# A gated state-space and feed-forward kernel: mirrored half of the forward transform taken from odd rows times -2, taps selected across column tiles, a third product buffer, PSUM banks given out by use, finer first loads, and a new order

## The chip, the cores and the metric

The kernel runs on one core of one Trainium2 chip. A core has five engines with a queue of instructions each: TensorE (PE, matrix products into PSUM), VectorE (DVE), ScalarE (ACT, functions from tables, copies, scalings), GpSimd (POOL) and SyncE (SP, here only transfers). An engine works through its own queue in order; engines wait for each other through semaphores. The metric is the device time of one execution in microseconds (us), less is better; a median of 3 runs is given.

## The reference

```python
x = A_u                                           # 1 x 2048 x 512, bf16
g = sigmoid((x * gate_w).sum(-1, keepdims=True))
# A: state-space convolution
dt = exp(log_dt)[:, None]
P = exp((dt * A)[:, :, None] * l)                 # A complex, D=512, N=128; l rounded to bf16
K = einsum("dn,dnl,dn->dl", C, P, dt * B).real    # one filter of 2048 taps per channel
a = irfft(rfft(pad(x)) * rfft(pad(K)))[:L] + x * Dskip
# B: the two rows with the largest x @ w_r go through a gated feed-forward layer (F = 1792)
y = (silu(x_sel @ w_gate) * (x_sel @ w_up)) @ w_down * sigmoid(r_sel)
b = x with y added at those two rows
out = g * a + (1 - g) * b
```

## The kernel before

The convolution is done in blocks of 1024 tokens with transforms written as matrix products. The 512 channels are worked in two halves, h = 0 and 1, of 256; tokens in two blocks, 0 and 1.

- **Parameters and tables.** The six parameter arrays are transposed on PE (`ptr`, line 612), and DVE makes from them the exponents `AL`, the angles `B16`, and the weights `WW` (this needs `PBR`, an eviction, line 494). `exps1` and `exps2` (lines 645 and 649) are exponentials on ACT for both halves. `trig` (line 654) makes four angles at a time: four scalings into integer arguments (`SCL`, line 498), a sine on ACT, an integer add (line 668), a cosine on ACT, and in `tab1` a negation. Arguments and sines each have two buffers. `tab1` and `tab2` (lines 674, 684) are done once per half; `tab2` ends with 12 products of 768 or 1792 columns.
- **Routing.** `routing` (line 717) transposes all tokens in 8 steps (line 724, evicted by line 494 as `XT`), computes gate and routing logits, picks two rows, and runs the feed-forward layer.
- **Forward transform.** `forward` (line 835): per block four frequency tiles `ft`. A first pass (`pm` 0) sums 4 even and 4 odd row tiles, an eviction follows, and a second pass (`pm` 1) adds four matmuls into the same PSUM with a matrix that is the odd one times -2 (`NG`, loaded eight times, 256 KB each), so that the mirrored frequencies come out; a second eviction follows.
- **Filter taps.** `kgen` (line 856) multiplies tables into taps `KA` in groups of six (one PSUM bank each), then selects taps with 32-column matmuls into `KC`. `kspec` (line 903) transforms the taps to `KK`.
- **Products and inverse.** `products` (line 929) multiplies the spectra on DVE, 2048 or 1024 columns at a time; block 1 also needs block 0's spectrum, and its products are written over the block's own spectrum (`xv(1)`). `inverse` (line 960) transforms back, line 992 scales, and SP stores.

Operations that two engines can do (`SCL`, `EV`, the add, the last scaling) are created with both variants, ACT first, except the add, which has DVE first. The string `ORDER` holds three characters per operation, its number in base 36, for all operations in a global order; each engine's queue is that order cut down to its own operations. The string `SECOND` holds a 0 or a 1 per operation; `fixed` (line 179) takes the engine from it:

```python
        for k, i in enumerate(seq):
            o = self.ops[i]
            if o.alt is not None:
                e = list(o.alt)[int(second[i])]
```

`emit` then derives each wait from what was read and written, for buffers that share memory too. PSUM's eight banks have fixed roles: two pairs for `forward` and `kspec`, two banks for `kgen`, two for the rest.

## Time and profile before

| | |
|---|---|
| median of 3 runs | 172.38 us (172.3 to 172.5) |
| span of the profiled execution | 170.1 us (its own time is not given; the median stands 2.3 us above its span) |
| DVE busy | 154.1 us, 248 instructions |
| PE busy | 149.8 us, 1686 matmuls |
| ACT busy | 123.8 us, 196 instructions |
| moved by DMA | 20.12 MB |
| ACT at work without larger gaps | 7.56 to 88 us |
| first DVE work, last DVE product's end | 6.84 us, 162.4 us |

The profile is one execution, taken by the hardware profiler. Its first part gives each engine's busy time, its share of the span and the number of instructions. The second cuts the span into 40 slices; a digit is the busy share of a slice in tenths. The chain follows the work that ended last back from the end, step by step, to what released it. Groups are rows of line, engine, operation, output and input shapes, count, busy time, mean time of one in ns, and idle time in front with what ended it. Many operations are recorded at the line of the helper that makes them: line 479 is `TT` (two tensors on DVE), 494 `EV` (evictions), 498 `SCL`, 490 `AC` (functions on ACT), 501 `DMA`. In a timeline the columns are start and length in us. Instructions of one engine overlap a little, so the step from start to start is shorter than a row's mean.

### The profile page before, as it was taken

The page shows a single profiled execution, that of the slowest core. Times are in us where ns is not written, and L with a number is a line of the kernel's source. Part 1 is how long each engine was busy: PE and PEld are TensorE (multiplying, and loading weights), DVE is VectorE, ACT ScalarE, POOL GpSimd, SP SyncE. Part 2 cuts the span into 40 slices and gives each one's busy share as a digit, 9 for nine tenths or more (in the row PEclk, how much of TensorE's full clock was granted, in tenths as well). Part 3 has the DMA queues.
Part 4 walks back from the last instruction along what each step waited for, and adds up shares of the span by engine and source line. Part 5 has one row for each costly group of instructions (what it writes and reads, how often), then busy time and mean ns, then how long its engine had stood idle before and what let it go on. Part 6 is the DMA issues. An engine that isn't in the chain of part 4 may idle for free.

```text
span 170.1 us, 3961 instructions
## 1 busy us (share of the span) xinstructions
PE 149.8 (88%) x1686; PEld 106.4 (63%) x1686; DVE 154.1 (91%) x248; ACT 123.8 (73%) x196; POOL 3.2 (2%) x8
## 2 busy tenths in 40 slices
PE   0607899989998999999988999999999999969980
PEld 0506674435753444778536779957888887858870
DVE  0399999999999999999999999999999999999931
ACT  2499999999999999999995567755765434506152
POOL 0002000000000000000000000030000000000000
PEclk9999999999999999999999999999999999999998
DMA  4999999273001101103904000049000020020514
GB/s 102 283 388 404 402 409 381 91 241 127 0 5 61 62 11 55 42 24 89 394 14 126 1 2 4 4 85 401 21 4 0 0 62 4 21 72 0 162 57 123
DMA packets 13411, 20.12 MB, mean 118 GB/s; under 512 B 1993, under 2 KB 9034, under 8 KB 13266
## 3 DMA queue, kind: packets, MB, share of 16 engines
q1 hardware_dynamic: 11906, 19.48, 32.5%
q10 hardware_dynamic: 1488, 0.40, 1.2%
q8 instruction: 13, 0.21, 0.5%
q14 instruction: 4, 0.03, 0.1%
HBM read 17.77 MB, written 2.10 MB: 117 GB/s over the span
## 4 chain that ended last, share of the span: by engine, by line
DVE 44%; ACT 23%; PE 22%; issue 6%; DMA 2%; SPq 0%
DVE AR L479 38%; ACT AR L490 14%; PE ps L850 9%; ACT AR L494 5%; PE ps L915 5%; PE ps L867 3%; DVE AR L494 2%; DMA AR<-c_bf 2%; ACT L255 2%; DVE AR L498 2%; PE ps L984 2%; PE ps L815 2%; ACT AR L498 1%; DVE AR L668 1%; DVE AR L488 1%
## 5 line engine op out<-in xcount | busy, mean ns | idle before, releaser
L479 DVE TENSOR_TENSOR AR<-AR 128x2048 bf16<-128x2048 bf16 (+8 forms) x138 | 118.2, 902 | 1.2
L494 ACT ACTIVATE AR<-ps 128x1024 bf16<-128x1024 f32 (+5 forms) x57 | 44.4, 803 | 19.0 <-PE ps L915 7.6
L490 ACT ACTIVATE AR<-AR 128x512 bf16<-128x512 f32 (+4 forms) x74 | 51.1, 753 | 2.5 <-DVE AR L479 1.9
L850 PE MATMUL ps<-AR 128*128 128x512 bf16 x192 | 44.3, 379 | 0.6 <-ACT AR L494 0.5
L984 PE MATMUL ps<-AR 128*128 128x256 bf16 x256 | 30.8, 273 | 2.0 <-DVE AR L479 1.9
L850 PEld LDWEIGHTS ps<-AR 128*128 128x128 bf16 x192 | 18.0, 99 | 22.2 <-issue 2.5
L984 PEld LDWEIGHTS ps<-AR 128*128 128x128 bf16 x256 | 24.8, 98 | 5.9 <-DVE AR L479 3.0
L992 ACT ACTIVATE AR<-ps,AR 128x256 bf16<-128x256 f32 x31 | 13.5, 473 | 18.5 <-PE ps L984 18.1
L915 PE MATMUL ps<-AR 128*128 128x256 bf16 x160 | 19.8, 273 | 0.7 <-ACT AR L494 0.7
L867 PEld LDWEIGHTS ps<-AR 128*128 128x128 bf16 x512 | 18.6, 98 | 1.3 <-ACT AR L494 0.3
L867 PE MATMUL ps<-AR 128*128 128x84 bf16 (+1 forms) x512 | 19.0, 198 | 0.1
L915 PEld LDWEIGHTS ps<-AR 128*128 128x128 bf16 x160 | 15.0, 98 | 5.3 <-ACT AR L494 2.3
L724 PE MATMUL ps<-AR 128*128 128x128 bf16 x64 | 7.7, 309 | 5.8 <-DVE AR L479 5.0
L498 DVE TENSOR_SCALAR AR<-AR 128x256 int32<-128x256 f32 (+1 forms) x38 | 11.0, 315 | 0.0
L724 PEld LDWEIGHTS ps<-AR 128*128 128x128 bf16 x64 | 6.3, 140 | 7.1 <-issue 6.3
L498 ACT ACTIVATE AR<-AR 128x256 int32<-128x256 f32 (+1 forms) x24 | 9.2, 438 | 0.0
L612 PE MATMUL ps<-AR 128*128 128x128 bf16 x24 | 2.9, 312 | 5.8 <-DMA AR<-c_bf 5.8
L971 PE MATMUL ps<-AR 128*128 128x256 bf16 x32 | 7.8, 273 | 0.1
L972 PE MATMUL ps<-AR 128*128 128x256 bf16 x32 | 7.7, 273 | 0.0
L479 DVE TENSOR_TENSOR AR<-AR,ps 128x512 f32<-128x512 bf16 x2 | 1.3, 684 | 6.8 <-PE ps L612 6.8
L494 DVE COPY AR<-ps 128x1024 bf16<-128x1024 bf16 x9 | 6.6, 743 | 0.4 <-PE ps L724 0.3
L612 PEld LDWEIGHTS ps<-AR 128*128 128x128 bf16 x24 | 2.4, 145 | 6.1 <-DMA AR<-c_bf 5.8
(49 smaller groups left out, 91.8 us busy)
## 6 DMA issues: line engine op xcount, KB each, us to landing
AR<-c_ksp SPq DMA_DIRECT2D x5, 512.0 KB, 4.9
AR<-in_A_u_dram SPq DMA_DIRECT2D x2, 1024.0 KB, 8.5
AR<-c_fwdn SPq DMA_DIRECT2D x8, 256.0 KB, 3.7
AR<-c_fwd SPq DMA_DIRECT2D x4, 512.0 KB, 11.4
AR<-c_inv SPq DMA_DIRECT2D x1, 2048.0 KB, 7.7
out_dram<-AR SPq DMA_DIRECT2D x16, 128.0 KB, 2.2
AR<-in_B_w_up_dram SPq DMA_DIRECT2D x1, 1792.0 KB, 15.4
AR<-in_B_w_gate_dram SPq DMA_DIRECT2D x1, 1792.0 KB, 17.9
```

The source lines that it names most:

```text
L479: return P.op(DVE, lambda h: h.tensor_tensor(out=o, in0=a, in1=b, op=op), rd, wr, cost=tt_cost(o, a, b), **k)
L490: return P.op(ACT, lambda h: h.activation(out=o, in_=a, func=func, scale=scale, bias=bias), rd, wr, cost=0.185 + nel(o) * 0.833e-3 + (0.09 ...
L494: return P.op((ACT, DVE), (lambda h: h.activation(out=o, in_=a, func=ACTF.Copy), lambda h: h.tensor_copy(o, a)), rd, wr, cost=(0.185 + n * ...
L498: return P.op((ACT, DVE), (lambda h: h.activation(out=o, in_=a, func=ACTF.Copy, scale=c), lambda h: h.tensor_scalar(out=o, in0=a, scalar1= ...
L724: last = h.transpose(bb(0, 128, db * 256 + t_ * 128, (1, 128)), U(0, 128, (2 * q + t_) * D + db * 128, (1, 128)), IDN(0, (1, 128)))
L850: last = h.matmul(o, w, U(0, 128, (blk * 8 + st * 2 + par) * D, (1, D)), start=(pm + par + st == 0), stop=(par == 1 and st == 3), skip_gro ...
L867: last = hh.matmul(pb(0, 128, (g - b0) * W4 + o, (1, n)), TP[h][1 - i // 2](0, 128, g * 128, (1, 128)), r[i](0, 128, g * n, (1, n)), start ...
L915: last = hh.matmul(pb(0, 128, n * 256, (1, 256)), KP[u](0, 128, tau * 128, (1, 128)), KC[h](0, 128, jg * 256, (1, 256)), start=(k == 0 and ...
L971: hh.matmul(pb(0, 128, e * 256, (1, 256)), DG(0, 128, tb[e] * 128, (1, 128)), U(0, 128, tb[e] * D + h * HC, (1, HC)), start=(e == 0), stop ...
L972: last = hh.matmul(pb(0, 128, e * 256, (1, 256)), OHR(0, 128, tb[e] * 128, (1, 128)), ZB(0, 128, h * HC, (1, HC)), start=False, stop=False)
L984: last = hh.matmul(pb(0, 128, e * 256, (1, 256)), G(0, 128, ((par * 2 + part) * 4 + ft) * 512 + (2 * t2 + e) * 128, (1, 128)), X(0, 128, h ...
L992: P.op((ACT, DVE), (lambda hh, o=o, i_=i_, g_=g_: hh.activation(out=o, in_=i_, func=ACTF.Copy, scale=g_), lambda hh, o=o, i_=i_, g_=g_: hh ...
```

## The change

- **Forward.** The `NG` matrices and their eight loads go. Instead `UO` holds the odd row tiles of a block times -2, made by one `SCL` of 2048 columns per block, and the second pass multiplies the odd matrix `F` with it. Evictions are as before.
- **Tap selection.** The loop over the four column tiles is moved inside, so that neighbouring matmuls go to different column tiles. `sel3` goes: its eight matmuls become part of `sel2` and write into its bank. `kgen` evicts two banks at a time (1008 columns, 6 evictions per half instead of 11).
- **Products.** Products for block 1 no longer overwrite `xv(1)`: each has a buffer of its own, from four places (h = 0) or five (h = 1).
- **Places.** A new class `Life` stands for one use of a PSUM bank, an argument or sine buffer or a product buffer; the string `PLACES` says which one it gets, and `fixed` adds waits between successive uses.
- **First loads.** U comes in four loads instead of two. The gate weights come as two contiguous loads on SP's queue and are transposed on PE (`w8`), where two element-wise loads on ACT's queue brought them; a DVE copy follows.
- **Smaller ones.** The down projection is turned round (56 matmuls of 2 columns for 14 of 512), with a small copy and four transposes behind it. The exponential of zero is a memset on POOL. `DG` reads its scale in pairs.
- **Order.** `ORDER` and `SECOND` are new (643 operations instead of 654); the list scheduler that had once made them is deleted, and lines 183 to 186 stay as they were.

As the code reads the strings, operations with two engines are placed so:

| operation | before: ACT, DVE | after: ACT, DVE |
|---|---|---|
| arguments, 256 | 23, 31 | 46, 8 |
| integer adds, 1024 / 768 | 4, 10 / 2, 0 | 3, 11 / 0, 2 |
| negations, 1024 | 1, 7 | 6, 2 |
| `XT` evictions, 1024 | 0, 8 | 7, 1 |
| `PBR` eviction, 1024 | 0, 1 | 1, 0 |
| forward evictions, 1024 | 12, 4 | 15, 1 |
| x(-2), 2048 | none | 1, 1 |
| `KA` evictions | 21, 1 | 10, 2 |
| `KC` / `KK` evictions | 6, 0 / 16, 0 | 5, 1 / 16, 0 |
| last scaling, 256 | 31, 1 | 29, 3 |

```diff
+class Life:
+    def __init__(self, prog, pool, n, home, region, name):
...
+        self.unit = int(PLACES[k], 36) if k < len(PLACES) else 0
+        self.base, self.c0 = home(self.unit)
+        self.alias = region.alias if region is not None else []
...
+            at[i] = k
             order[o.eng].append(o)
...
 SECOND = (
-    "000000000000000000000000000000001000000000000000000000000000000000000000000000000001010101010101010000000000000000000000000000000000000000000000000000"
...
+    "000000000000000000000000000010000000000000000011001011011100110011100000101010000000010000000000000000000000000000000000000000000000000010100000101000"
+    "001011001001001000010010000000000100100000000101010000000000000011001001000001010000000100000000010000000000000000000000000001001000000000000000000000"
+    "001000000101001000010000001101010000000000000000010110000000000000000000001000000000000000000000000000000000000000000000000000000000000000000000000000"
     "000000000000000000000000000000000000000000000000000000000000000000000000000000000000000000000000000000000000000000000000000000000000000000000000000000"
...
+    "0000000000000000000000000000000100010100000"
+)
+PLACES = (
+    "002423114301111116067020011001126404066110011002421322011010010110010446000024606464021213003203021666446420013427241030132344032571064"
 )
...
+        used = {}
+        for l in self.lives:
+            for u in range(l.unit, l.unit + l.n):
+                used.setdefault((l.pool, u), []).append(l)
+        for ls in used.values():
+            ls.sort(key=lambda l: min(at[i] for i in l.all))
+            for a, b in zip(ls, ls[1:]):
+                assert max(at[i] for i in a.all) < min(at[i] for i in b.all), "a place is held twice"
+                for i in b.all:
+                    self.ops[i].deps.update(a.all)
...
-        NG = [B("ng%d" % i, oF + 16 * KB + 2 * i * KB, 2 * KB) for i in range(2)]
+        UO = B("uo", oF + 16 * KB, 4 * KB)
...
-        PQ = [[B("p%d%d" % (i, h_), o + 4 * i * KB, 4 * KB) for i in range(2)] for h_, o in enumerate((oTI[0], oI))]
+        PQR = [B("pq%d" % h_, o, n * KB) for h_, (o, n) in enumerate(((oTI[0], 16), (oI, 20)))]
+        def place(pool, region, off, nbytes, dt=BF):
+            def home(u):
+                a = AR[:, (off + u * nbytes) // 2:(off + (u + 1) * nbytes) // 2]
+                return (a if dt == BF else a.bitcast(dt)), 0
+            return Life(P, pool, 1, home, region, pool)
...
-            DQ([(U(0, 128, j * 8 * D, (2 * D, 4), (1, 2 * D)), dr(A_u, 1024 * j * D, (2 * D, 128), (256 * D, 4), (1, 2 * D)))], [], [(U, (t, h_)) for t in range(8 * j, 8 * j + 8) for h_ in range(2)], 1048576)
+            for k in range(2):
+                DQ([(U(0, 128, (j * 8 + k * 4) * D, (2 * D, 2), (1, 2 * D)), dr(A_u, (1024 * j + 512 * k) * D, (2 * D, 128), (256 * D, 2), (1, 2 * D)))], [], [(U, (t, h_)) for t in range(8 * j + 4 * k, 8 * j + 4 * k + 4) for h_ in range(2)], 524288)
...
-                if j == 0:
-                    DQ([(NG[ft](0, 128, 0, (1, 1024)), ngsrc(ft))], [], [NG[ft]], 262144)
-        P.op(ACT, ld_w, [], [WL], cost=1.0, n=2, nbytes=20000, dma=True, prio=2.5e5)
+        for i, w in enumerate((gate_w, B_w_r)):
+            DQ([(W8(4 * i, 4, 0, (1, 128)), dr(w, 0, (128, 4), (1, 128)))], [], [(W8, i)], 1024)
...
+            w8 = misc(True)
+            P.op(PE, lambda h: h.transpose(w8(0, 128, 0, (1, 8)), W8(0, 8, 0, (1, 128)), CB(0, 8, 0, (1, 8))), [(W8, 0), (W8, 1), CBI], [w8], cost=0.25)
+            CP(WL(0, 128, 0, (1, 8)), w8(0, 128, 0, (1, 8)), [w8], [WL])
...
-            yb = misc()
+            yb, yt = misc(), misc(True)
             def dn(h):
-                for fb in range(14):
-                    last = h.matmul(yb(0, 2, 0, (1, D)), HB(0, 128, 3 * 28 + fb * 2, (1, 2)), WD[fb // 8](0, 128, fb % 8 * D, (1, D)), start=(fb == 0), stop=(fb == 13))
+                for db in range(4):
+                    for fb in range(14):
+                        last = h.matmul(yb(0, 128, db * 2, (1, 2)), WD[fb // 8](0, 128, fb % 8 * D + db * 128, (1, 128)), HB(0, 128, 3 * 28 + fb * 2, (1, 2)), start=(fb == 0), stop=(fb == 13))
-            P.op(PE, dn, [(HB, 3), *WD], [yb.buf], cost=14 * 0.226)
-            CP(HY(0, 2, 0, (1, D)), yb(0, 2, 0, (1, D)), [yb.buf], [HY])
-            TS(ZB(0, 2, 0, (1, D)), HY(0, 2, 0, (1, D)), RTS(0, 2, 37, (1, 1)), MUL, [HY, K("rs"), (ZB, None)], [(ZB, "y")])
+            P.op(PE, dn, [(HB, 3), *WD], [yb], cost=56 * 0.0255)
+            CP(YT(0, 128, 0, (1, 8)), yb(0, 128, 0, (1, 8)), [yb], [YT])
+            def ytr(h):
+                for db in range(4):
+                    last = h.transpose(yt(0, 2, db * 128, (1, 128)), YT(0, 128, db * 2, (1, 2)), IDN(0, (1, 128)))
+            P.op(PE, ytr, [YT, CBI], [yt], cost=0.3)
+            TS(ZB(0, 2, 0, (1, D)), yt(0, 2, 0, (1, D)), RTS(0, 2, 37, (1, 1)), MUL, [yt, K("rs"), (ZB, None)], [(ZB, "y")])
...
+                SCL(UO(0, 128, 0, (1, 4 * D)), U(0, 128, (blk * 8 + 1) * D, (2 * D, 4), (1, D)), -2.0, uk(*range(blk * 8 + 1, blk * 8 + 8, 2)), [UO])
                 for ft in range(4):
-                    k = blk * 4 + ft
-                    ng = NG[k % 2]
-                    if k > 1:
-                        DMA([(ng(0, 128, 0, (1, 1024)), ngsrc(ft))], [], [ng], 262144, prio=2e5)
-                    pb = fwp[k % 2]
+                    pb = psum(2)
                     for pm in range(2):
                         for part in range(2):
-                            def fw(h, blk=blk, ft=ft, pm=pm, pb=pb, ng=ng, part=part):
+                            def fw(h, blk=blk, ft=ft, pm=pm, pb=pb, part=part):
                                 last = None
                                 o = pb(0, 128, part * 512, (1, 512))
                                 for par in range(pm, 2):
                                     for st in range(4):
-                                        w = ng(0, 128, (st * 2 + part) * 128, (1, 128)) if pm else F(0, 128, ft * 2048 + ((par * 4 + st) * 2 + part) * 128, (1, 128))
-                                        last = h.matmul(o, w, U(0, 128, (blk * 8 + st * 2 + par) * D, (1, D)), start=(pm + par + st == 0), stop=(par == 1 and st == 3), skip_group_check=(pm == 1))
+                                        w = F(0, 128, ft * 2048 + ((par * 4 + st) * 2 + part) * 128, (1, 128))
+                                        x = UO(0, 128, st * D, (1, D)) if pm else U(0, 128, (blk * 8 + st * 2 + par) * D, (1, D))
+                                        last = h.matmul(o, w, x, start=(pm + par + st == 0), stop=(par == 1 and st == 3), skip_group_check=(pm == 1))
                                 return last
-                            P.op(PE, fw, ([ng] if pm else [(F, ft)]) + uk(*range(blk * 8, blk * 8 + 8)), [(pb.buf, part)], cost=(8 - 4 * pm) * 0.217)
...
-            for b0 in range(0, 64, 6):
-                ng = min(6, 64 - b0)
-                pb = kgp[(b0 // 6) % 2]
+            for b0 in range(0, 64, 12):
+                ng = min(12, 64 - b0)
+                pb = psum(1 + (ng > 6))
                 W4 = 4 * NJ
-                def mm(hh, b0=b0, ng=ng, pb=pb):
...
+                for g0 in range(0, ng, 6):
+                    def mm(hh, b0=b0, gs=range(g0, min(ng, g0 + 6)), pb=pb):
+                        last = None
+                        for g in gs:
+                            for i in range(4):
+                                n, o = (W4, 0) if i % 2 == 0 else (4 * NR, 4 * NOF)
+                                last = hh.matmul(pb(0, 128, g // 6 * 512 + g % 6 * W4 + o, (1, n)), TP[h][1 - i // 2](0, 128, (b0 + g) * 128, (1, 128)),
+                                                 r[i](0, 128, (b0 + g) * n, (1, n)), start=(i == 0), stop=(i == 3))
+                        return last
+                    P.op(PE, mm, [*TP[h], *r], [(pb, g0)], cost=min(6, ng - g0) * 4 * 0.0343)
+                d = ((512, ng // 6), (1, 6 * W4)) if ng > 6 else ((1, ng * W4),)
+                EV(KA[h](0, 128, b0 * W4, (1, ng * W4)), pb(0, 128, 0, *d), [pb], [(KA[h], b0)])
...
                 def sel(hh, bk=bk, pb=pb):
                     last = None
-                    for k in range(4):
+                    for c4 in range(4):
+                        for k in range(4):
+                            last = hh.matmul(pb(32 * k, 32, c4, (256, 2), (4, 64)), CB(0, 128, c4, (4, 32)), ka(c4, GROUPS[2 * bk][k], (16, 2)),
+                                             start=(c4 == 0), stop=(c4 == 3 and bk + k > 0), tile_position=(0, 32 * k))
+                    if bk == 0:
                         for c4 in range(4):
-                            last = hh.matmul(pb(32 * k, 32, c4, (256, 2), (4, 64)), CB(0, 128, c4, (4, 32)), ka(c4, GROUPS[2 * bk][k], (16, 2)),
-                                             start=True, stop=(bk + k > 0), tile_position=(0, 32 * k))
-                            if bk + k == 0:
-                                last = hh.matmul(pb(0, 32, c4, (4, 64)), CB(0, 128, 64, (1, 32)), ZB(0, 128, h * HC + c4, (4, 64)), start=False, stop=True, tile_position=(0, 0))
+                            last = hh.matmul(pb(0, 32, c4, (4, 64)), CB(0, 128, 64, (1, 32)), ZB(0, 128, h * HC + c4, (4, 64)), start=False, stop=(c4 == 3), tile_position=(0, 0))
                     return last
...
-            pb, pe = misc(), misc()
+            pb = misc()
             def sel2(hh):
                 last = None
-                for k in range(4):
+                for c4 in range(4):
+                    for k in range(4):
+                        last = hh.matmul(pb(32 * k, 32, c4, (4, 64)), CB(0, 128, c4, (4, 32)), ka(c4, GROUPS[4][k]), start=(c4 == 0), stop=(c4 == 3 and k != 1), tile_position=(0, 32 * k))
+                for k in range(2):
                     for c4 in range(4):
-                        last = hh.matmul(pb(32 * k, 32, c4, (4, 64)), CB(0, 128, c4, (4, 32)), ka(c4, GROUPS[4][k]), start=True, stop=True, tile_position=(0, 32 * k))
...
-            PA, PBb = PQ[h]
+            nbytes = 8 * W
+            tmp = lambda: place("pq%d" % h, PQR[h], (oTI[0], oI)[h], nbytes)
+            halves = lambda b: [(b, 0), (b, 1)]
             for blk in blks:
-                for P_, part in ((PA, 0), (PBb, 1)):
-                    TT(v4(P_), xv(blk), kv(0, part), MUL, kx(blk) + kk(0, part), [P_])
+                pq = [tmp(), tmp()]
+                for part in range(2):
+                    TT(v4(pq[part]), xv(blk), kv(0, part), MUL, kx(blk) + kk(0, part), halves(pq[part]))
                 if blk == 1:
-                    for P_, part in ((PA, 0), (PBb, 1)):
-                        TT(xv(1), xv(0), kv(1, part), MUL, kx(0) + kk(1, part), kx(1))
-                        TT(v4(P_), v4(P_), xv(1), ADD, kx(1), [P_])
-                TT(v1(PA, 0), v1(PA, 0), v1(PBb, 1), SUB, [PBb], [PA])
-                TT(v1(PA, 1), v1(PA, 1), v1(PBb, 0), ADD, [PBb], [PA])
+                    for part in range(2):
+                        t = tmp()
+                        TT(v4(t), xv(0), kv(1, part), MUL, kx(0) + kk(1, part), halves(t))
+                        TT(v4(pq[part]), v4(pq[part]), v4(t), ADD, halves(t), halves(pq[part]))
+                PA, PBb = pq
+                TT(v1(PA, 0), v1(PA, 0), v1(PBb, 1), SUB, [(PBb, 1)], [(PA, 0)])
+                TT(v1(PA, 1), v1(PA, 1), v1(PBb, 0), ADD, [(PBb, 0)], [(PA, 1)])
```

## The prediction

> **What bounds the kernel now.** I read the page's busy table and slices first, then the table by stage, the groups kept apart by shape, the chain, and ACT's timeline.
>
> ```profile
> span 170.1 us, 3961 instructions
> ...
> PE 149.8 (88%) x1686; PEld 106.4 (63%) x1686; DVE 154.1 (91%) x248; ACT 123.8 (73%) x196; POOL 3.2 (2%) x8
> ...
> DVE  0399999999999999999999999999999999999931
> ACT  2499999999999999999995567755765434506152
> ...
> DVE 44%; ACT 23%; PE 22%; issue 6%; DMA 2%; SPq 0%
> ```
>
> DVE is the bound from 6.84 us to 162.4 us. ACT is just as full in the first 21 slices, to about 88 us; its 27% of idle time lies behind that. What goes onto ACT early costs time, what goes onto it late is free.
>
> ```profile
> core 0: us, PE busy (x) PEld busy (x) DVE busy (x) ACT busy (x) POOL busy (x), PEclk, DMA share, GB/s
> ...
> 69.00:88.00 19.00, 18.17 (x310) 12.54 (x307) 18.79 (x31) 18.92 (x31) 0.00 (x0) 1.00 0.35 126
> 88.00:105.40 17.40, 16.66 (x226) 13.04 (x225) 17.32 (x21) 11.00 (x15) 0.00 (x0) 1.00 0.11 32
> ...
> 162.50:170.10 7.60, 3.63 (x32) 3.01 (x32) 0.99 (x2) 3.10 (x7) 0.00 (x0) 0.92 0.26 75
> ```
>
> ACT's timeline gives the step from one instruction to the next: eviction of 1024 0.90 us, sine 0.95, argument 0.31, integer add 0.94.
>
> ```profile
> 43.57 1.00 ACT L494 ACTIVATE AR<-ps 128x1024 bf16<-128x1024 f32 x1
> 44.47 1.04 ACT L490 ACTIVATE AR<-AR 128x1024 bf16<-128x1024 int16 x1
> 45.42 0.40 ACT L498 ACTIVATE AR<-AR 128x256 int32<-128x256 f32 x1
> 45.73 1.04 ACT L668 ACTIVATE AR<-AR 128x1024 int32<-128x1024 int32 x1
> ...
> 84.95 1.78 ACT L490 ACTIVATE AR<-AR 128x1024 bf16<-128x1024 int16 x2
> ```
>
> The last row ends with the last cosine of the second half's tables, at 86.6 us (the next eviction starts at 86.63). Behind it DVE has the rest of that table, then all products, with no gap.
>
> **Where the work lands.** Line 186, which picks the engine of each operation that has two, is not in the diff, so it still reads SECOND by the operation's number. The old string has 59 ones, all on two-engine operations by number. The new one has 61: by number only 22 fall on two-engine operations (171 of 643 are such, so chance gives 16), but by place in ORDER all 61 do. The new string is therefore written by place and read by number, and the engines come out almost at random. Counted through ORDER, ACT gets, up to and with that last cosine:
>
> - arguments 46 instead of 23: 23 x 0.31 = +7.1
> - seven of the eight transposed-input evictions (L494, 1024 from PSUM) that DVE does today: 7 x 0.91 = +6.4, and the P eviction +0.9
> - negations 6 instead of 1: 5 x 0.95 = +4.8
> - forward evictions 14 instead of 9: 5 x 0.91 = +4.6
> - the first new x(-2) of 2048 elements: rows of 256 (411 ns) and 1024 (1056 ns) give 0.84 ns an element, so 1.9, in steps 1.8
> - table evictions: 2 of 1008 (1.8) for 9 of 504 (0.49 steps) and one of 336 (0.4): -3.0
> - adds -1 of 1024 and -2 of 768: -2.5; one exponential less (the memset is on POOL): -0.5
>
> Sum +19.6 us, none of it beside anything: ACT is full there.
>
> **New waits on ACT in that stretch.** (1) The P eviction stands behind seven exponentials (7.56 + 7 x 0.53 = 11.3, done 12.2). DVE's CM2 waits for it, B16 stands behind CM2, and ACT's first argument waits for B16 to 14.0: 1.8. (2) The 12 products of the first half's second table start only when DVE has passed the integer add of a sine that ACT reaches at about 79; they take 10.5, the first two table matmul groups 48 x 0.037 = 1.8, and the eviction that now stands on ACT behind them waits 3.4. (3) Two forward evictions wait for PE, which was held by the down projection and its new transposes: 1.5. (4) Two cosines wait for adds that went to DVE: 0.5 and 1.4. Together 8.6; ends 0 (all caught by slack) and 13 (half as much again). The last cosine ends at 86.6 + 19.6 + 8.6 = 114.8.
>
> **Behind it.** Two table evictions 1.3. Then the three selection groups. Today 16 matmuls of 128 columns are 1.4 us (64 are 5.6), the groups with additions 1.9 and 1.4: 4.7 with no overlap. With neighbours in different column tiles, at best a quarter: 1.2. No row shows it; I take 3.0 and keep both ends. The small eviction ahead of DVE's work went to DVE: 0.4. DVE goes on at 119.5. It still has a cosine product, four of 1024 and a TS, 3.3 in steps; then 8 of 1792 (1.04) and 4 of 768 (0.54), 10.5. Products: today they and DG run from 101.1 to 162.5, 61.4. Dependent neighbours are 1.26 apart (143.74, 145.00, 146.25), independent ones 1.13 (41.46 to 42.59) and 0.61 for 1024. With a third buffer and the new order hardly any neighbours depend on each other: 33 x 1.13 + 32 x 0.61 + 0.8 = 57.5; I take 58.0, ends 57.5 and 61.4. KK evictions stay 2 to 3 us ahead of the products that read them by the same walk, so no wait there. Tail: 162.46 to 170.1 is 7.6; one of the four last inverse groups (32 matmuls 3.67, so 0.9) now stands before DVE's last product: 6.7.
>
> Sum: 119.5 + 3.3 + 10.5 + 58.0 + 6.7 = **198.0 us** of span against 170.1. The profiled execution's own time is not given beyond its span; the median of the runs, 172.38, lies 2.3 above it, so **200.3 us**.
>
> **Parts at nothing.** The eight mirrored-matrix loads (2 MB): no row of PE waits for them; the price if their absence mattered is nil, as DMA was busy for 0.03 to 0.35 between 40 and 105. Four loads of U and two of gate weights (SP, 0.45 each to issue) hide behind ACT's first seven exponentials; w8's transpose blocks the third parameter transpose to about 8.2, still before 11.3 (without that cover the transposes would start some 2 us late, as U's first load takes 7.4 to land today). The down projection: 14 x 0.23 = 3.2 becomes 56 x 0.028 + 0.3, which is on today's chain, but PE then waits for ACT: nothing. The freed HY copy (0.67) and DG's paired reads (0 to -0.6) are on a DVE that waits or are small. PSUM by use: today's PSUM wait, 5.0 before the input transposes, is replaced by the wait for the P eviction. The second x(-2) (on DVE, at most twice the 0.42 of 1024) falls in DVE's idle time. SP's queue: KP's five loads (0.45 each to issue, 4.9 to land) can start when the last forward group is done, about 109, and are in by about 117.5; if they come later, DVE's 13.8 us of table work cover as much. G (7.7 to land) starts when the second half's table matmuls are done, about 142, and is in by 150, ahead of the first inverse group at about 155; without that room each us would hold PE alone. POOL's memset of OHR (1.8) and its load lie in the same gap. ACT's queue loses two gate-weight issues (0.98) that stood before its 3.2 us table load, while DVE's first result at 7.5 still sets its start.
>
> **Rules of the skill.** The trace grants PE a clock of 1.00 in all stages up to 162.5 us. The Trainium skill, "TensorE: Matmul & The Clock Gate" (Part 1), says that about 3.4 us of idleness halve PE's clock until about 3.4 us of work have passed; only the 0.92 of the last stage hints at that here. The Trainium skill, "TensorEngine Tiling (Array Packing)" (Theoretical Speedup), gives up to 4x for 32 columns: by it the sum would be 1.8 lower, by the old rows alone 1.7 higher.
>
> **Rivals.**
> - *Read by place after all*: if the string took effect as it fits, ACT's early load would be as now (31 arguments and all eight evictions on DVE). DVE's sum changes by: forward eviction -1.2, table eviction -0.65, add +0.6, negation +0.35, two x(-2) +1.3, HY and small ones -0.4: 0. Then 172.4 - 3.4 (products) - 0.9 (tail) = 168. Against it: line 186 is not in the diff. 5%.
> - *DVE's relief decides (the other side)*: read by number, DVE has 218 instructions for 248 and about 11 us less. If DVE is the bound throughout, 172.4 - 11 - 3.4 - 0.9 = 157. It decides only if ACT's last cosine ends by 172.0 - (200.3 - 114.8) = 86.5, which is today's 86.6; each us later is a us on the end. ACT would need 28 us of slack in front of 88, and the slices show none. 3%.
> - *PE goes cold*: PE would now idle for stretches of 5 to 12 us. At half clock the first table pair costs +1.8, the selections +3.0: 205. The clock column speaks neither way, as PE had no such gaps. 18%.
> - *A part of the moves hides* (some waits and a third of the moves, 175 to 189): 5%. *More stalls than I found*, such as KK late for the second half: over 213, 7%.
>
> **How the numbers follow.** The forecast as summed has 62%. Low end: no new waits (-8.6), selections 1.2 (-1.8), products 57.5 (-0.5): 189. High end: waits +4.3, selections +1.7, products +3.4, cold PE's rest +3: 213. With the cold case inside, that holds 80%. What a measurement here can tell from no change is 0.2%, 0.35 us. Faster: 5% + 3% = 8%; the same 1%; slower 91%.
>
> **What would show it.** Right: the exponentials end near 48 us instead of 36.8; ACT full to about 115 with some 46 L498-type instructions on it; DVE's busy share well under 80%, its idle time ended by ACT between 35 and 119; products packed from about 133 to 191; ACT nearly idle behind 150. Wrong: DVE as full as now before 100 us, or eight transposed-input evictions on DVE (then the string is read by place); PE's clock at half in many stages (the cold case); a wait of DVE for KK evictions.

## The result and the profile after

The changed kernel takes 206.8 us (median of 4 runs, 206.4 to 207.2) against 172.3 us for the kernel before in the same comparison: a ratio of 1.200, with a 95% interval of 1.198 to 1.203. It is 34.5 us slower; 200.3 had been forecast, with a range of 189 to 213. The profiled execution has a span of 204.8 us against 170.1. An execution that lies over 1.5% above the fastest of its kernel, at a lower clock granted to PE, is left out of the ratios: one of four with extra matmuls in part 2 (209.7 us) and three of four with three classes by place in part 4 (196.9 to 197.8 us).

From the page of the changed kernel: span, busy table, the slices of DVE, ACT and PE's clock, and the shares of the chain.

```profile
span 204.8 us, 4017 instructions
...
PE 152.9 (75%) x1718; PEld 109.7 (54%) x1733; DVE 141.6 (69%) x218; ACT 141.0 (69%) x218; POOL 3.6 (2%) x10
...
DVE  0456010640588679597984846999997999999952
ACT  3566999999889898488999853822686654351153
...
PEclk9999975597599597999999959997999999999999
...
PE 39%; ACT 37%; DVE 18%; issue 2%; DMA 2%; SPq 0%; ACTq 0%; DVEq 0%
```

DVE was at 9 in nearly every slice before. Now it stays at 9 only behind slice 25 (with one 7); ahead of that it has holes, and it is busy 141.6 us for 154.1. ACT has gone from 123.8 to 141.0 us, all of it in front: there it works 20.3 us more (below), behind that 3 us less. The chain's largest share was DVE's 44%; it is now split between PE (39%) and ACT (37%). ACT's part lies almost wholly ahead of 120 us; from 138 us to the end the chain lies on PE nearly throughout.

The line of the engine choice is 137 in this kernel (186 before); `TT` is line 436, `AC` 447, `EV` 451, `SCL` 455, the integer add 610. The next rows are ACT's timeline in the changed kernel (start, length, and in brackets the idle time in front and what ended it).

```profile
14.23 0.42 ACT L455 ACTIVATE AR<-AR 128x256 int32<-128x256 f32 x1 [1.96 <-DVE AR L436]
...
18.78 5.61 ACT L451 ACTIVATE AR<-ps 128x1024 bf16<-128x1024 bf16 x6 [1.70 <-PE ps L666]
...
25.14 9.47 ACT L447 ACTIVATE AR<-AR 128x512 bf16<-128x512 f32 x18
...
49.56 4.37 ACT L455 ACTIVATE AR<-AR 128x2048 bf16<-128x2048 bf16 x7
...
86.99 1.02 ACT L451 ACTIVATE AR<-ps 128x1024 bf16<-128x1024 f32 x1 [2.97 <-PE ps L800]
...
118.49 0.84 ACT L447 ACTIVATE AR<-AR 128x768 bf16<-128x768 int16 x1 [1.48 <-DVE AR L610]
```

The transposed-input evictions stand on ACT in front of 18 exponentials, x(-2) and arguments follow the last exponential at 49.6, and the last cosine ends at 119.3 us, where it ended at 86.6 before. That is 32.7 of the 34.7 us by which the span has grown. Behind it, DVE's timeline:

```profile
124.36 0.42 DVE L451 CAST AR<-ps 128x256 bf16<-128x256 f32 x1 [4.06 <-PE ps L847]
...
128.03 9.97 DVE L436 TENSOR_TENSOR AR<-AR 128x768 bf16<-128x768 bf16 x12
...
155.09 42.04 DVE L436 TENSOR_TENSOR AR<-AR 128x2048 bf16<-128x2048 bf16 x50
```

DVE goes on 5.1 us behind the cosine, starts the 12 table products at 128.03 and ends the last product at 197.13; the remaining 7.7 us are the tail. The same view by stage as before, here from ACT's first exponential to its last cosine (first the kernel before, then the changed one in two rows; the columns are those of the table by stage above):

```profile
7.56:86.63 79.07, 71.83 (x808) 42.88 (x810) 77.67 (x160) 78.81 (x125) 1.17 (x3) 1.00 0.48 177
```

```profile
7.00:49.66 42.66, 22.43 (x185) 13.46 (x185) 14.24 (x46) 38.33 (x64) 0.31 (x1) 0.83 0.61 226
49.66:119.30 69.64, 54.83 (x641) 31.42 (x649) 53.35 (x83) 60.76 (x93) 0.00 (x0) 0.87 0.06 21
```

Before, ACT worked 78.8 of 79.1 us. Now it works 38.3 + 60.8 = 99.1 us of the 111.7 between 7.62 and 119.3: 20.3 us more work, and 12.3 us more waiting.

### The profile page after: what moved, and what is told of

The parts are those of the page before. It is cut to its first block, busy times and chain, and to the rows that moved or that the text cites. A ratio compares the mean times of both kernels' runs of the same rounds, so it can differ in the third digit from the quotient of the medians.

```text
span 204.8 us, 4017 instructions
## 1 busy us (share of the span) xinstructions
PE 152.9 (75%) x1718; PEld 109.7 (54%) x1733; DVE 141.6 (69%) x218; ACT 141.0 (69%) x218; POOL 3.6 (2%) x10
## 4 chain that ended last, share of the span: by engine, by line
PE 39%; ACT 37%; DVE 18%; issue 2%; DMA 2%; SPq 0%; ACTq 0%; DVEq 0%
ACT AR L447 21%; DVE AR L436 15%; PE ps L934 13%; ACT AR L451 7%; ACT AR L455 6%; PE ps L818 6%; PE ps L864 4%; PE ps L800 4%; PE ps L831 2%; DMA AR<-in_A_A_im_dram 2%; PE ps L922 2%; PE ps L921 2%; PE ps L666 2%; ACT AR L610 1%; ACT L217 1%
## 5 line engine op out<-in xcount | busy, mean ns | idle before, releaser
L436 DVE TENSOR_TENSOR AR<-AR 128x1024 bf16<-128x1024 bf16 (+6 forms) x138 | 115.3, 891 | 12.8 <-ACT AR L455 10.3
L451 ACT ACTIVATE AR<-ps 128x1024 bf16<-128x1024 f32 (+6 forms) x56 | 51.4, 956 | 30.4 <-PE ps L871 12.0
L800 PE MATMUL ps<-AR 128*128 128x512 bf16 x182 | 51.2, 440 | 9.7 <-ACT AR L455 7.5
L800 PEld LDWEIGHTS ps<-AR 128*128 128x128 bf16 x192 | 20.5, 111 | 35.1 <-issue 11.8
L934 PE MATMUL ps<-AR 128*128 128x256 bf16 x256 | 29.4, 273 | 0.0
L934 PEld LDWEIGHTS ps<-AR 128*128 128x128 bf16 x256 | 25.0, 98 | 2.9
L942 ACT ACTIVATE AR<-ps,AR 128x256 bf16<-128x256 f32 x29 | 12.3, 474 | 18.7 <-PE ps L934 17.6
L455 ACT ACTIVATE AR<-AR 128x256 int32<-128x256 f32 (+2 forms) x53 | 23.7, 510 | 2.0 <-DVE AR L436 2.0
L818 PEld LDWEIGHTS ps<-AR 128*128 128x128 bf16 x512 | 19.3, 101 | 10.0 <-DVE AR L436 6.9
L864 PE MATMUL ps<-AR 128*128 128x256 bf16 x160 | 18.8, 273 | 0.2 <-ACT AR L451 0.2
L864 PEld LDWEIGHTS ps<-AR 128*128 128x128 bf16 x160 | 15.2, 98 | 3.6 <-ACT AR L451 0.7
L610 DVE TENSOR_SCALAR AR<-AR 128x1024 int32<-128x1024 int32 (+1 forms) x11 | 7.3, 665 | 6.3 <-ACT AR L447 6.3
L831 PE MATMUL ps<-AR 128*32 128x128 bf16 x64 | 4.2, 421 | 6.7 <-ACT AR L451 6.7
L557 PE MATMUL ps<-AR 128*128 128x128 bf16 x24 | 3.1, 310 | 6.1 <-DMA AR<-in_A_A_im_dram 5.8
L921 PE MATMUL ps<-AR 128*128 128x256 bf16 x32 | 7.5, 272 | 0.0
L922 PE MATMUL ps<-AR 128*128 128x256 bf16 x32 | 7.5, 272 | 0.0
L666 PE MATMUL ps<-AR 128*128 128x128 bf16 x64 | 5.7, 265 | 2.3 <-ACT AR L451 2.3
L451 DVE CAST AR<-ps 128x1008 bf16<-128x1008 f32 (+2 forms) x4 | 4.0, 1011 | 4.1 <-PE ps L847 4.1
## 6 DMA issues: line engine op xcount, KB each, us to landing
AR<-in_B_w_up_dram SPq DMA_DIRECT2D x1, 1792.0 KB, 13.8
```

The costliest lines, as they stand in the source:

```text
L436: return P.op(DVE, lambda h: h.tensor_tensor(out=o, in0=a, in1=b, op=op), rd, wr, cost=tt_cost(o, a, b), **k)
L451: return P.op((ACT, DVE), (lambda h: h.activation(out=o, in_=a, func=ACTF.Copy), lambda h: h.tensor_copy(o, a)), rd, wr, cost=(0.185 + n * ...
L455: return P.op((ACT, DVE), (lambda h: h.activation(out=o, in_=a, func=ACTF.Copy, scale=c), lambda h: h.tensor_scalar(out=o, in0=a, scalar1= ...
L666: last = h.transpose(bb(0, 128, db * 256 + t_ * 128, (1, 128)), U(0, 128, (2 * q + t_) * D + db * 128, (1, 128)), IDN(0, (1, 128)))
L800: last = h.matmul(o, w, x, start=(pm + par + st == 0), stop=(par == 1 and st == 3), skip_group_check=(pm == 1))
L818: last = hh.matmul(pb(0, 128, g // 6 * 512 + g % 6 * W4 + o, (1, n)), TP[h][1 - i // 2](0, 128, (b0 + g) * 128, (1, 128)), r[i](0, 128, (b ...
```

## The experiments

Each ratio is to the kernel before, measured beside the kernel in question. Where two experiments are set against each other, I take the difference of their ratios times 172.4 us; the changed kernel's ratio is 1.2003.

**1. Is it the reading of the string?** The string is read by place in `ORDER` instead of by operation number. First throughout, then for the places up to the last cosine alone (the first 376), then for those behind it alone.

```diff
-                e = list(o.alt)[int(second[i])]
+                e = list(o.alt)[int(second[k])]                        # throughout
+                e = list(o.alt)[int(second[k if k < 376 else i])]      # early
+                e = list(o.alt)[int(second[i if k < 376 else k])]      # late
```

> The changed kernel with one index changed: the engine string is read by place in the order, as it fits. Theory (ACT's load ahead of the last cosine sets the end): ACT's last cosine back to 85 to 88 us, DVE the bound again, 166 to 171 us against 172.3 before. Rival A (the parts of the change themselves, such as the x(-2) step, the waits between successive uses of a place or the new order, make half of the loss or more): 188 us or more. Rival B (mostly PE's low clock in gaps): the gaps stay where the new order makes them, 190 to 200.

> The changed kernel, engines by place for the first 376 places of the order (up to and with the last cosine), by number behind it. Theory: nearly all of the loss goes, what is left is table and selection evictions put on DVE behind the cosine, 1 to 4 us: 168 to 174. Rival (the assignment as a whole, late part too): about half way, 185 to 190.

> The other way round: by number up to the last cosine, by place behind it. Theory: the loss stays, 203 to 207 against 206.8 for the change. Rival (the assignment as a whole): about half way, 185 to 190.

Measured: throughout 170.55 us (ratio 0.987, 0.984 to 0.991); early 175.5 (1.019); late 200.9 (1.166). One character of the source is worth 36.7 us of 172.4, and with it the rest of the change leaves the kernel 1.3% below the one before, a small gain whose interval stays below 1. So this kernel beats both, and the loss is the reading of the string and nothing else. The early part is worth 31.2 us, the late part 6.0, together 37.2. The early one came out a little above what had been expected, and the late one was mis-sized (203 to 207 had been expected): two evictions that by number fall to DVE, a table eviction of 1008 and the small one of 256 behind the selections, stand in DVE's queue ahead of the table products. Read by number, these start 8.7 us after the last cosine (119.3 to 128.03), read by place 3.4 us; with the late part alone by place it is 3.4 us too, with the early part alone 8.8. In the kernel read by place, from its timelines of ACT and DVE:

```profile
88.66 2.23 ACT L451 ACTIVATE AR<-ps 128x1008 bf16<-128x1008 f32 x3
```

```profile
15.71 4.27 DVE L451 COPY AR<-ps 128x1024 bf16<-128x1024 bf16 x7
...
92.13 9.97 DVE L436 TENSOR_TENSOR AR<-AR 128x768 bf16<-128x768 bf16 x12
```

The transposed inputs are evicted by DVE, all three remaining table evictions are on ACT, and DVE walks past them to the products.

**2. Is a cold PE part of it?** PE's granted clock in the changed kernel is 0.73 to 0.81 between 20 and 84 us. 97 matmuls of 512 columns, whose results nothing reads, were put into PE's longest waits. The strings were renumbered for these four operations; the engine and the order of all others stay.

```diff
+        for n_ in [34, 30, 7, 26]:
+            pb = psum(1)
+            def warm(h, pb=pb, n_=n_):
+                last = None
+                for _ in range(n_):
+                    last = h.matmul(pb(0, 128, 0, (1, 512)), U(0, 128, 0, (1, 128)), U(0, 128, 0, (1, 512)), start=True, stop=True)
+                return last
```

> The changed kernel with 97 extra matmuls of 512 columns in four of PE's long waits (34 before the first transpose of the routing maximum, 30 before the first mirrored pass, 7 before the down projection, 26 before the selections); they read U and write a free PSUM bank that nothing reads. Theory: PE then runs at full clock where the changed kernel had 0.6 to 0.8, forward evictions come earlier, 2 to 5 us less than the change: 202 to 205. Rival C (the low clock is off the path): 206.3 to 207.5. Rival B (the low clock is most of the loss): under 195.

Measured: the mean clock rises from 0.90 to 0.95, and the time is 205.8 us (205.0 to 206.7; ratio 1.194, 1.188 to 1.200); the span is 203.2 for 204.8. So this warming brought 1.1 us by the ratios (2.5 at the ends of their intervals) and 1.6 in span: below the 2 to 5 that the theory had, with a time between the theory's range and rival C's. PE was not warm throughout, as between 20 and 84 us the clock rose from 0.76 to 0.89 only; what full warmth would bring was not measured. The selections, for which the cold rival had added 3.0 us, show why it is little: their first 32 matmuls take 2.11 us at a clock of 1.00 here, and 2.09 at 0.50 in the changed kernel. The matmuls that do slow down (eight of 512 columns take 3.54 us behind the idle stretch that ends at 38.2 us, and the next eight 1.89) lie where ACT is busy anyway (14.96 of the 15 us from 35 to 50). The Trainium skill, "TensorE: Matmul & The Clock Gate" (Part 1), says that a PE idle for about 3.4 us runs at half clock until it has worked as long; the trace agrees, 0.44 us a matmul behind 9.7 us of idleness and 0.24 later. Not every such gap does it here: in the kernel before PE is idle for 4.99 us until 13.73, and the clock granted behind it is 1.00.

**3. Does each us on ACT count?** One class at a time was set right in the changed kernel: the arguments, or the transposed-input and P evictions.

```diff
-                e = list(o.alt)[int(second[i])]
+                e = list(o.alt)[int(second[k if o.name[0][0] == "arg" and o.cost < 0.4 else i])]                      # arguments
+                e = list(o.alt)[int(second[k if o.name[0][0][:2] == "xt" or o.name[0][0] == "pbr" else i])]           # evictions
```

> The changed kernel with the engine of the arguments alone read by place: 23 of them go from ACT to DVE ahead of the last cosine. Theory (each us of ACT ahead of the last cosine is a us at the end): 23 x 0.31 = 7.1 less, 206.8 to 199.7, between 198 and 202. Rival (ACT only waits longer, as DVE's small operations now stand in front of its integer adds and products): 203 to 208.

> The changed kernel with the engine of the transposed-input evictions and of the P eviction alone read by place: seven and one go back to DVE. Theory: 7 x 0.91 + 0.9 = 7.3 of ACT work and the wait for B16 (2.0) and for the input transposes (1.7) go: 206.8 - 11.0 = 195.8, between 194 and 199. Rival as for the arguments: 203 to 208.

Measured: 204.9 us (ratio 1.185, so 2.7 less) and 203.3 us (1.178, 3.9 less), for 7.1 and 7.3 us of work taken from ACT. The last cosine came 2.0 and 4.1 us earlier. Both times lie in the rival's range. The rule that had carried the forecast, that each us on ACT early is a us at the end, fails here by about half or more. In the first kernel ACT waits 4.45 us for PE at the first table eviction, for 0.66 in the changed one, and 5.8 us for DVE in three places where it had waited 2.1. ACT's timeline of the second kernel shows what replaced the work:

```profile
19.09 1.02 ACT L451 ACTIVATE AR<-ps 128x1024 bf16<-128x1024 f32 x1 [6.27 <-PE ps L800]
```

By number, one eviction of the forward transform (block 0, `ft` 1, first pass; it stands at place 72 of `ORDER`, and by place it is DVE's) stands on ACT in front of 18 exponentials. ACT waits 6.3 us there for a product that PE can only make once the transposes are through. In the changed kernel the wait does not show, because the misplaced input evictions fill that very time.

**4. Three more tests of that.** First three classes at once: arguments, transposed-input and P evictions, negations and x(-2) by place; forward and table evictions and adds still by number. Then the reverse: everything by place except the arguments, and everything except the transposed-input and P evictions.

```diff
-                e = list(o.alt)[int(second[i])]
+                e = list(o.alt)[int(second[k if o.name[0][0][:2] == "xt" or o.name[0][0] in ("pbr", "snc", "uo") or o.name[0][0] == "arg" and o.cost < 0.4 else i])]   # three classes
+                e = list(o.alt)[int(second[i if o.name[0][0] == "arg" and o.cost < 0.4 else k])]                      # all but the arguments
+                e = list(o.alt)[int(second[i if o.name[0][0][:2] == "xt" or o.name[0][0] == "pbr" else k])]           # all but the evictions
```

> The changed kernel, in which the arguments, the input-transpose and P evictions, the negations and the two x(-2) are read by place together; forward and table evictions and the adds stay by number. Counted through ORDER with the steps of the trace of before, this takes 22 us of work from ACT ahead of the last cosine (46.4 to 24.5 in these classes, and by place in full it is 25.2). Arguments alone gave 1.9 and the evictions alone 3.5. Theory A (the loss is shared by several queues, and one class set right only uncovers waits on the next, so that the gains together are much more than their sum): last cosine before 100, 178 to 188. Theory B (the gains simply add, 1.9 + 3.5 + 2 to 3 for the negations and x(-2)): 197 to 200. Theory C (each us of ACT's work counts in full, 22 in all): about 185, last cosine near 97; A and C are told apart by the single moves, which C had at 7.1 and 7.3 and which gave 1.9 and 3.5.

> All read by place, but the arguments by number: ACT gets 23 arguments more ahead of the last cosine, 7.1 us in steps; the rest is as in the kernel read by place throughout (170.55 us). Theory (where ACT is full and the other queues are in step, as before 88 us there, each us put on it counts): last cosine at 94 to 97 instead of 88.75, 175.5 to 178.5. Rival (a class that gave only 1.9 when it was set right alone costs no more when it alone is wrong): 171.5 to 173.5.

> All read by place, but the input-transpose and P evictions by number: seven of eight and the P eviction on ACT, 7.3 us of work in front of and among ACT's exponentials, and DVE's early parameter work then waits for the P eviction behind seven exponentials. Theory: last cosine at 95 to 98, 176.5 to 179.5. Rival (only what it gave when set right alone, 3.5): 173 to 175.

Measured: three classes 193.1 us in the one execution that is compared, 196.9 to 197.8 in the three others; all but the arguments 176.8 (ratio 1.027, 1.022 to 1.031); all but the evictions 181.5 (1.056, 1.050 to 1.061).

The three classes together gained 13.8 us in the execution that is compared (9 to 10 in the others) for 22 us of work. That is short of theory C, the full price, and of theory A, whose last cosine was to come before 100 us and comes at 108.78. Theory B (the gains add) had 197 to 200: the three others lie at its lower end, the compared one 4 us below it. So the full price is not reached; whether the gains only add or come to somewhat more is open. The table by stage, from the first exponential to the last cosine, shows where the rest is. The profile of the second kernel is of the execution that took 196.9 us, so up to 3.8 us of what follows may be its own. First row: read by place throughout; second: three classes by place; third: all but the arguments.

```profile
7.60:88.75 81.15, 72.41 (x821) 42.64 (x829) 77.52 (x164) 77.61 (x119) 0.39 (x1) 0.91 0.35 127
```

```profile
7.80:108.78 100.98, 75.93 (x822) 44.84 (x829) 77.98 (x167) 77.35 (x118) 0.39 (x1) 0.85 0.29 105
```

```profile
7.60:96.10 88.50, 73.07 (x822) 42.02 (x829) 74.00 (x142) 84.48 (x142) 0.31 (x1) 0.90 0.33 119
```

ACT has the same work in the first two, 77.6 and 77.4 us, and DVE too (77.5 and 78.0), and yet the second takes 20 us longer: ACT idles 23.6 us for 3.5. The loss is all waits now, and two rows of ACT's timeline hold 13.6 us of them; the third row is DVE's:

```profile
19.69 1.02 ACT L451 ACTIVATE AR<-ps 128x1024 bf16<-128x1024 f32 x1 [8.05 <-PE ps L800]
...
88.44 1.01 ACT L451 ACTIVATE AR<-ps 128x1008 bf16<-128x1008 f32 x1 [5.59 <-PE ps L818]
```

```profile
32.56 0.17 DVE L441 TENSOR_SCALAR AR<-AR 128x16 bf16<-128x16 f32 x1 [9.38 <-ACT AR L447]
```

The first is the same forward eviction. The exponentials end 9 us later than in the kernel read by place, and DVE, whose next operation reads a result that ACT has behind 18 of them, stands 9.4 us for it. The second is the first table eviction: it waits for PE, PE waits for DVE's table products, and these stand behind everything that DVE does late. A kernel with these forward evictions set right as well was not run, so how much of the 20 us is that one instruction's is open; its own wait is 8.

The reverse tests give the full price, and more. With 23 arguments on ACT, 7.1 us in steps, its busy time rises by 6.9 us (77.6 to 84.5), the last cosine comes 7.3 us later, and the span is 7.3 us longer (176.0 for 168.7); by the ratios it is 6.7 us, inside the 175.5 to 178.5 expected. The evictions cost 11.7 us by the ratios and 10.5 in span for 7.3 us of work, above the 176.5 to 179.5 expected. The rest is two new waits in ACT's timeline of that kernel, 2.05 + 1.13 = 3.2 us for the transposes on PE:

```profile
14.27 1.94 ACT L451 ACTIVATE AR<-ps 128x1024 bf16<-128x1024 bf16 x2 [2.05 <-PE ps L666]
...
17.34 4.69 ACT L451 ACTIVATE AR<-ps 128x1024 bf16<-128x1024 bf16 x5 [1.13 <-PE ps L666]
```

So the same 23 arguments cost about 7 us where all else is in step, and give back 2 to 4 where it is not. The price of a misplaced class is real when it is the only one; several of them stand in each other's shadow.

**5. What are the intended parts worth?** In the kernel read by place, the products of block 1 were again written over the block's own spectrum, with the old order of the six operations and no third buffer. In the changed kernel, the selection loops were put back.

```diff
-                        t = tmp()
-                        TT(v4(t), xv(0), kv(1, part), MUL, kx(0) + kk(1, part), halves(t))
-                        TT(v4(pq[part]), v4(pq[part]), v4(t), ADD, halves(t), halves(pq[part]))
+                        TT(xv(1), xv(0), kv(1, part), MUL, kx(0) + kk(1, part), kx(1))
+                        TT(v4(pq[part]), v4(pq[part]), xv(1), ADD, kx(1), halves(pq[part]))
...
-                    for c4 in range(4):
-                        for k in range(4):
+                    for k in range(4):
+                        for c4 in range(4):
```

> The changed kernel read by place, but with the block 1 products written over the block's own spectrum as in the kernel before, and the six operations of each such group in the old order (two products, then product, sum, product, sum). Theory: dependent neighbours are 0.13 apart more, 5 a group, 4 groups: 2.6 more than by place (170.6), so 172 to 174. Rival (the third buffer buys nothing, other work hides the steps): 170 to 171.2.

> The changed kernel with the tap selections looping over the column tiles outside again. In the changed kernel the first half's selections stand between the last cosine's table evictions and DVE's next work, 120.72 to 124.36 us. Theory: they take 0.55 us a group longer (1.4 for 1.07), two to three groups, 1 to 2 us on the end: 207.8 to 209. Rival (PE's low clock there hides it, or another engine is later): 206.3 to 207.3.

Measured: products in place 171.6 us against 170.55 (ratios 0.9934 and 0.9874, so 1.0 us; the intervals touch, so it is hardly clear of noise), between the 172 to 174 expected and the rival's 170 to 171.2. The last product ends 2.6 us later (163.75 for 161.15): 1.3 us in the packed stretches of products, and the rest in a longer wait for an eviction of `KK` ahead of them. Not all of it reaches the end (the spans differ by 1.9 us), as in the kernel read by place the chain lies on PE for the most part:

```profile
PE 70%; DVE 18%; ACT 5%; DMA 2%; issue 2%; SPq 0%; ACTq 0%
```

With the old selection loops the ratio is 1.199 (1.197 to 1.201) against 1.200: no difference that these runs can tell. Their first 32 matmuls take 2.13 us in the old order and 2.09 in the new one, all three groups 3.85 and 3.53, so the spread over column tiles brings about 0.3 us at most here. The theory's 0.55 us a group came from setting a group alone (17 matmuls in 1.36 us in the kernel before, of which the last one's own length is 0.42) against half of a row of 32. From start to start the old order takes 59 ns a matmul there and 55 here, the new one 54. The 207.8 to 209 of the theory did not come, and the rival, 206.3 to 207.3, holds.

**6. A still faster version?** In the kernel read by place, POOL took both x(-2) and the arguments that ACT has behind 53 us (21 of them, two more than the expectation counted).

```diff
+                if e == ACT and o.name[0][0] == "arg" and o.cost < 0.5 and k > 214:
+                    o.eng, o.fn = POOL, o.alt[DVE][0]
...
-                SCL(UO(0, 128, 0, (1, 4 * D)), U(...), -2.0, uk(...), [UO])
+                P.op(POOL, lambda h, blk=blk: h.tensor_scalar(out=UO(0, 128, 0, (1, 4 * D)), in0=U(...), scalar1=-2.0, scalar2=None, op0=ALU.mult), uk(...), [UO], cost=2.0)
```

> All read by place; the two x(-2) of 2048 elements on POOL, and the 19 arguments that are on ACT behind 53 us on POOL too, which has no work there (POOL is busy 3.7 us in all). It takes 19 x 0.31 = 5.9 us from ACT, and 1.2 us and a wait of 1.7 us for PE from DVE. The profile shows no such operation on POOL, so its price is open. Theory: the last cosine comes 1 to 4 earlier and with it the products, 167 to 169.5. Rival (POOL is slow at these, above 0.6 us an argument, and the sines wait for it, or DVE runs slower beside it): 170.5 or more.

Measured: 188.0 us (ratio 1.090), 17.7 us slower than without POOL. The groups of POOL and two rows of the timelines of POOL and DVE (line numbers are two higher in this kernel):

```profile
L457 POOL TENSOR_SCALAR AR<-AR 128x256 int32<-128x256 f32 x21 | 32.4, 1543 | 44.5 <-ACT AR L449 43.6
L790 POOL TENSOR_SCALAR AR<-AR 128x2048 bf16<-128x2048 bf16 x2 | 10.7, 5361 | 0.0
```

```profile
15.07 5.36 POOL L790 TENSOR_SCALAR AR<-AR 128x2048 bf16<-128x2048 bf16 x1
```

```profile
15.29 5.48 DVE L457 TENSOR_SCALAR AR<-AR 128x256 int32<-128x256 f32 x2
```

An argument takes 1.54 us on POOL on average, for a step of 0.31 on ACT, and ACT waited up to 11.0 us for them. And POOL holds DVE up: two arguments that DVE otherwise does in 0.48 us last as long as POOL's x(-2) beside them. The rival holds.

## Why the prediction was right, and where its sizes were off

The sign, the cause and the range held; the time was 6.5 us above the forecast. The cause, line 186 reading by number a string written by place, is shown by the one-character edit. Its first rival, read by place after all, had been given 168 us; that kernel, once made, measures 170.55. Where it erred is the sizes, and what bounds the end. Term by term, predicted and measured:

- **Work put on ACT early**: +19.6, measured +20.3 (78.8 to 99.1). Right.
- **New waits on ACT**: 8.6, measured 12.3. This term was mis-sized, and its parts more than its sum. The P eviction cost 1.96 for 1.8 and the two waits for adds 0.55 and 1.48 for 0.5 and 1.4, as walked. But the wait for table matmuls was 0.66 for 3.4 and the forward evictions' waits for PE 4.0 (2.97 + 1.05) for 1.5, and not in the list were the wait for the input transposes, 1.70, and three short ones for DVE and PE, 2.1 together. That one part was 2.7 too high and others some 6 too low, so that the sum is 3.7 off, is in part luck. The last cosine came at 119.3 instead of 114.8: 4.5 of the 6.8 us by which the span was missed.
- **Behind the cosine**: DVE on after 4.7, measured 5.4; the selections took 3.6 for the 3.0 taken, inside the ends kept. The upper end, 4.7, added up groups timed alone; in a row, even the old order takes 3.85. The 3.3 was right, the 10.5 measured 10.0.
- **Products**: 58.0 (its terms add to 57.6, not 57.5), measured 59.1, of which 1.18 is a wait for a `KK` eviction. The text had held that there would be no wait there. The gain from the third buffer, put at 3.4, is 1.0 in time and 2.6 at the last product.
- **Tail**: 6.7, measured 7.7. No gain came from an inverse group ahead of DVE's last product: the sum had taken DVE for the only bound there. The rows below (the stage that ends with DVE's last product, first the kernel before, then the changed one) show PE's share: 10.56 of 12.50 us before, 21.10 of 21.10 now. PE runs its last 96 matmuls of the inverse back to back from 190.32 to 200.96 us, where before it had waited for DVE.
- **The difference of time and span**: 2.3, measured 2.0.

```profile
150.00:162.50 12.50, 10.56 (x95) 8.74 (x93) 12.16 (x16) 3.35 (x8) 0.00 (x0) 1.00 0.27 79
```

```profile
176.00:197.10 21.10, 21.10 (x196) 18.90 (x195) 21.07 (x27) 8.44 (x21) 0.00 (x0) 1.00 0.18 50
```

Sum of the misses: 4.5 + 0.7 - 0.5 + 1.1 + 1.0 = 6.8 us, 198.0 to 204.8.

One step of the reasoning was weaker than it looked. "What goes onto ACT early costs time" is right for an ACT that is full with its neighbours in step: there 7.1 us of arguments cost 6.7 to 7.3. As an account of the changed kernel it is no sum of prices: taking 22 us of that work away again gained 9 to 14. The total came out near because the forecast walked ACT's queue as a whole, with its waits, instead of pricing classes one by one, and because errors in single waits partly cancelled.

The cold PE had been given 18% and 205 us, and the time lies near that number; warming PE moved it by 1.1 us (2.5 at the ends of the intervals), so this rival is not the main reason. Its remark that PE had no such gaps before overlooks one of 4.99 us. DVE's relief (157 us) needed slack on ACT that was not there. Of the signs named in advance, these came: exponentials to 49.7 us (48 forecast), ACT at work for 99.1 of the 111.7 us up to 119, DVE's share at 69%, products packed from 138 to 197. ACT, called nearly idle behind 150, is at 1 to 6 tenths there. Of the signs against, two showed in part: DVE's wait of 1.18 us for a `KK` eviction, and a clock of 0.73 to 0.81 in the stages from 20 to 84 us.

## What to carry to other kernels

When a table of choices is changed, read the line that looks it up: an index that no longer fits its table gave a working kernel here, with its engines dealt out almost at random. On engines that work in order, price a moved class by walking the queue it lands in, waits included; a class that costs its full length in a kernel that is in step may cost little where others are misplaced, and setting one right only shows the next wait. And before believing that a part is worth nothing, undo the wrong part and measure it in the kernel without it.

## What was not expected of the hardware

- POOL is no spare engine for these operations: it takes 5.36 us for a scaling of 2048 columns that DVE does in 0.69, and beside that scaling DVE's operations stand (5.48 us for two that take 0.48; a product of 1024 columns took 4.13 us beside the second x(-2), for 0.68). The Trainium skill, "SBUF — State Buffer" (Who interferes with whom), says that POOL and DVE share a pair of ports, that in DVE's modes with two ports whoever issues first holds the pair for the whole instruction while the other waits, and that a DVE instruction with two inputs in SBUF contends with POOL's reads. The first row agrees; the second contends, but not for the whole instruction, as that product ended at 64.05, 1.2 us ahead of POOL's.
- Selections of 128 columns on 32-column tiles take 65 to 67 ns each in a row of 32, whether neighbours go to different column tiles (2.09 us for 32) or the same (2.13), and whether the granted clock is 0.50 (2.09) or 1.00 (2.11). What sets this time is open. The "up to 4x" that the prediction quoted from the Trainium skill, "TensorEngine Tiling (Array Packing)" (Theoretical Speedup), does not show here.
